# Linear attention and SwiGLU, two layers: half the one-column products, three weight loads spread out, an early silu table

## The chip, the cores and the metric

One core of a Trainium2 chip. The metric is the device time of one execution in microseconds. All arithmetic on TensorE is in pairs of 16-bit numbers (a high and a low part of each fp32 value), three matmuls for one product.

## The reference

x has 2048 rows (tokens) of 512. Two layers follow each other, with the same weights; each is

```python
x = x + A(layernorm(x))        # linear attention, 32 heads of 16
x = x + B(layernorm(x))        # out = (silu(x w1) * (x w3)) w2, F = 1792

# A:
phi = lambda t: where(t > 0, t + 1, exp(t)) + 1e-6
pq, pk = phi(q), phi(k)
kv = einsum("bhsd,bhse->bhde", pk, v);  z = sum of pk over the rows s
o  = (pq @ kv) / (pq . z + 1e-6)
return o @ wo
```

## The kernel before

The work goes through 16 token tiles of 128 rows. A layer has four stages.

*Keys* (the loop over t in `attention`). For each tile, `mm(pp, ...)` makes the keys (12 matmuls into the bank pk) from the transposed, normalised rows `xts[t]`; ACT and DVE make phi of it (`phi_act`, `phi_sum`), ACT rounds its high part (L942), DVE takes the low part (L957); and `gram(t)` adds rows-times-keys to four banks gt (12 matmuls). `keys_turn(t + 3)` splits the normalised rows of tile t + 3 (POOL or DVE, L1136) and has a DMA transpose write `xts[t + 3]` (L1137); `keep_transposed` stores one tile earlier to xt_d (L1155). POOL makes the layernorm's scale of tile t + 4.

*State*. The string `STATE[layer]` lists, in order, the steps between keys and queries: `totals` and `inverse` (the sum of the keys in the bank pz; its power-of-two inverse rz, L388), `gram_j` (gt times rz, L995, and its high part on ACT, L996), `low_j` and `lowp_j` (low parts on DVE or POOL, L999), `z` (zb, a scaled copy of pz, L1002), `col` (turns rows into columns by matmuls against a vector one_row that has a one in its first place, and makes from them the factor col), `kv`, `kvs` (kv masked and split, L1044 to L1054), `m_j` (kvs times wo, scaled by col, the weights that the queries' results meet; L1066, L1067), and the first queries `q_t`, `phi_t`, `in_t`, `out_t`.

*Queries*. The string `LOOP[layer]` lists the steps of each tile t from 0 to 13; `a` adds the attention's result to x and takes the row sums for the next layernorm (L1234, and on ACT L1238 and L1239). The last two tiles are added in the first group of the MLP.

*MLP*. Groups of Strassen-like products (banks ba, bb, bc), silu on ACT (L1288), the hidden values' parts, and products into the banks po. In layer 0 its idle slots also prepare the weights.

Between the layers (the seam), layer 1's first key tiles run among the last products of layer 0's MLP: `before_gram(t)` is `second(t)`, which for t = 0 and 1 closes the MLP, and at t = 1 loads layer 1's attention weights wv, wq and wo from att_d (1 MB each, L1705 to L1707).

The order on every engine is the order in which the code emits it (`in_order` pins PE, DVE, ACT, POOL and SP); every DMA goes through SP's one queue. ACT holds one set of functions at a time; exp and silu are in different sets, and the build puts an ACT_TABLE_LOAD ahead of the first activation that needs the other.

`f32()` hands out short-lived rows from a ring of four, in turn.

Of the kernel before, what the change touches and what calls it, by code (L numbers as in the profile page):

```python
# [11 lines left out]
AF = mybir.ActivationFunctionType  # L12
OP = mybir.AluOpType
# [4 lines left out]
P = 128  # L18
S, D, F, H = 2048, 512, 1792, 32
DH = D // H  # L20
NT, NC, NK, NF = S // P, S // 512, D // P, F // P
# [50 lines left out]
class Ring:  # L72
# [5 lines left out]
    def next(self, dtype, *dims):  # L78
        at = self.offsets[self.n % len(self.offsets)]
        self.n += 1  # L80
        return self.view(at, dtype, *dims)
# [7 lines left out]
def kernel(  # L89
# [10 lines left out]
    nc = tc.nc  # L100
# [10 lines left out]
    def view(at, dtype, *dims):  # L111
        size = 4 if dtype == F32 else 2
        n = size
        for d in dims:
            n *= d
        ap = arena[:, at // 4 : (at + n) // 4]
        if dtype != F32:
            ap = ap.bitcast(dtype)
        if len(dims) > 1:
            names = "abcdefg"[: len(dims)]  # L120
            ap = ap.rearrange(
                f"p ({' '.join(names)}) -> p {' '.join(names)}",
                **{n: d for n, d in zip(names[1:], dims[1:])},
            )
        return ap
# [36 lines left out]
    def f32(kind="short"):  # L162
        return ring[kind].next(F32, D)

    def later(n):
# [35 lines left out]
    LOADS = (  # L201
        (
            "q:2 b0:2 b1:3 b2:4 b3:5 v:6 o:7 b4:8 b5:9 b6:10 b7:11"
        ),
    )

    FIRST = (
# [14 lines left out]
    )  # L222
    LOOP = (
        (
            "f p i v f q w f o a"
        ),
        (
            "f p f q o i w v f a"
        ),
    )  # L230
    FILLS = (
# [76 lines left out]
    def scalar():  # L308
        i = next(column)
        return scalars[:, i : i + 1]  # L310

    one_row = scalar()
# [2 lines left out]
    small_eps = scalar()  # L315
    nc.vector.memset(small_eps, EPS * 2.0**-15)
    one_eps = scalar()
    nc.vector.memset(one_eps, 1.0 + EPS)

    mv_all = const.tile([P, NT, 2], F32, name="mv_all")  # L320
# [8 lines left out]
    wv_s = view(XB1, F16, 2, NK, D)  # L329
    wq_s = view(AT_H + 7 * KB, F16, 2, NK, D)  # L330
    wo_s = view(AT_H + 15 * KB, F16, 2, NK, D)
    g_s = view(XB0, F16, 2, NK, D)
    m_s = view(XB1, F16, 2, NK, D)
    zb = view(XB1 + 8 * KB, F32, D)
# [13 lines left out]
    att_d = {n: dram.tile([P, 2, NK, D], F16, name=f"{n}_d") for n in "kvqo"}  # L348
# [81 lines left out]
    def settle():  # L430
        while owed:
            owed.pop(0)()
# [12 lines left out]
    info = {}  # L445
# [434 lines left out]
    def attention(layer, ready, prep, before_gram):  # L880
# [5 lines left out]
        gt, pz, pks = [], [], {}  # L886
# [92 lines left out]
        held = {}  # L979
# [20 lines left out]

        def keep_z():
            nc.scalar.activation(zb, pz[0], AF.Copy, scale=info["itk"])  # L1002

        def columns():

            col = columns_
            for src, at in ((zb, 0), (held["rz"], 4)):
                for c in range(NK):
                    nc.tensor.matmul(
                        pz[0][:, at + c : at + c + 1],  # L1010
                        src[:, c * P : (c + 1) * P],
                        one_row,
                        start=True,
                        stop=True,
                    )
            held["col"] = col
            nc.vector.tensor_copy(col, pz[0][:, :4])
            nc.vector.scalar_tensor_tensor(
                col,
                col,  # L1020
                info["tk"],
                pz[0][:, 4:8],
                OP.mult,
                OP.mult,
            )
            nc.vector.reciprocal(col, col)
            nc.vector.tensor_scalar(col, col, 2.0**-17, None, op0=OP.mult)

        def kv_products():
# [26 lines left out]
        def out_weights(c):  # L1056
# [17 lines left out]
            "totals": totals,  # L1074
            "inverse": inverse,
            "z": keep_z,
            "col": columns,
            "kv": kv_products,
            "kvs": kv_parts,
# [16 lines left out]
        def out_of(t):  # L1096
            pos[t] = attn_out(t)

        ticks = {
            "q": lambda t: 4 < t + 4 < NT and query(t + 4),  # L1100
            "o": out_of,
# [3 lines left out]
            "a": lambda t: attn_add(t, pos.pop(t)),  # L1105
            "f": lambda t: fill(prep),
            "v": lambda t: settle(),
        }
        for t in range(NT - AFTER):
            next_tick(prep)  # L1110
# [60 lines left out]
    def query(t):  # L1171
        xt = xqs.pop(t)
        pp = acc_bank("pq") if t >= DEEP else bank("pq")
        mm(pp, lambda a, k: xt[:, a * NK + k, :], lambda b, k: wq_s[:, b, k, :], NK)
        pqs[t] = phi_act(pp, info["uq"], False, t >= DEEP)
        if t + 3 < NT:
            load_query(t + 3)
# [48 lines left out]
    def attn_out(t):  # L1226
        pt = pts.pop(t)
        po = bank("po")
        mm(po, lambda a, k: pt[:, a * NK + k, :], lambda b, k: m_s[:, b, k, :], NK)
        return po  # L1230
# [410 lines left out]
    for item in LOADS[0].split():  # L1641
        what, t = item.split(":")
# [58 lines left out]
    def second(t):  # L1701
        if t < 2:
            pending(t)
        if t == 1:
            nc.sync.dma_start(wv_s, att_d["v"])  # L1705
            nc.sync.dma_start(wq_s, att_d["q"])
            nc.sync.dma_start(wo_s, att_d["o"])  # L1707

    pair(1, nxt, None, second)


# [31 lines left out]
```

## Time and profile before

| | |
|---|---|
| time, median of 3 runs | 1192.5 us (1191.66 to 1192.67) |
| the profiled execution | 1187.6 us, span 1185.9 us |
| mean granted clock | 0.995 |
| matmuls (L1009) of the step `col`, recorded passes | 32 in both layers, median 250 ns each |
| ACT_TABLE_LOAD | 4, 1283 ns each; two of them at silu (L1288) |
| loads of wv, wq, wo, issue to landing | 7.4, 10.1 and 11.8 us |
| transposes of L1137, issue to landing | least 3.0, median 3.6, most 8.8 us |

Times are microseconds from the start of the span. PE is TensorE's matmuls, SPq the queue of DMA issues. A bracket at a timeline row gives how long the engine was idle before it and what it waited for. An fp32 matmul shows as two passes.

### The profile page before, as it was taken

What the parts mean: (1) busy time and instruction counts of PE and PEld (TensorE: products, weight loads), DVE (VectorE), ACT (ScalarE), POOL (GpSimd) and SP (SyncE); (2) the same over time, 40 slices, a digit from 0 to 9 for tenths busy, and PEclk for the clock granted to TensorE, in tenths of its full rate; (3) what the DMA queues carried; (4) which work ended last, traced back from release to release, by engine and by line L of the source; (5) the groups of instructions that cost most, each with busy time, mean ns of one, the idle gap of its engine ahead of it and who ended that gap; (6) DMA issues with size and microseconds to landing.
All of it is one profiled execution on the core that took longest, in us unless ns stands there. A gap on an engine that the chain in (4) does not pass through costs nothing.

```text
span 1185.9 us, 21854 instructions
## 1 busy us (share of the span) xinstructions
PE 1153.6 (97%) x8884; PEld 867.1 (73%) x8884; DVE 832.3 (70%) x1385; ACT 638.3 (54%) x1076; POOL 418.5 (35%) x488
## 2 busy tenths in 40 slices
PE   8999998899999999999998999999999999999998
PEld 3445444788888888888863454468888888888887
DVE  6788898977977896757774559747755775756543
ACT  5787687856554454334456644765544444444422
POOL 5342588302000134235267714684532200102010
PEclk9999999999999999999999999999999999999999
DMA  8986565979532221112226435664351350120010
GB/s 260 341 224 222 132 160 107 265 241 297 160 137 98 82 81 63 63 63 72 73 91 140 107 104 104 127 147 120 103 131 71 125 187 14 68 81 37 1 37 36
DMA packets 163396, 147.43 MB, mean 124 GB/s; under 512 B 129632, under 2 KB 138976, under 8 KB 158688
## 3 DMA queue, kind: packets, MB, share of 16 engines
q1 hardware_dynamic: 163296, 146.04, 42.7%
q8 instruction: 69, 1.13, 0.4%
q14 instruction: 31, 0.25, 0.1%
HBM read 72.48 MB, written 42.07 MB: 97 GB/s over the span
## 4 chain that ended last, share of the span: by engine, by line
PE 66%; DVE 12%; DMA 7%; POOL 6%; ACT 5%; issue 2%; SPq 1%; POOLq 0%; ACTq 0%; DVEq 0%
PE bb L514 17%; PE po L1380 13%; PE bc L514 9%; PE gt L514 6%; PE pk L514 5%; PE pq L514 4%; DMA arena<-arena 4%; PE ba L514 4%; PE po L514 3%; PE po L1400 3%; DMA arena<-in_B_w_dram 3%; DVE arena L1289 2%; DVE arena L1294 1%; DVE arena L1336 1%; DVE arena L1429 1%
## 5 line engine op out<-in xcount | busy, mean ns | idle before, releaser
L514 PEld LDWEIGHTS <-arena 128*128 128x128 f16 x6360 | 619.8, 98 | 261.6 <-issue 17.8
L514 PE MATMUL bb<-arena 128*128 128x256 f16 x2688 | 331.6, 274 | 7.9 <-ACT arena L1333 5.7
L1380 PE MATMUL po<-arena 128*128 128x256 f16 x1932 | 234.6, 273 | 6.8 <-ACT arena L1292 4.0
L1380 PEld LDWEIGHTS <-arena 128*128 128x128 f16 x1932 | 187.9, 98 | 33.0 <-ACT arena L1292 7.1
L1294 DVE TENSOR_TENSOR arena<-arena 128x512 f16<-128x512 f32 (+1 forms) x104 | 115.1, 1107 | 105.6 <-ACT arena L1292 105.3
L1333 ACT ACTIVATE arena<-bb 128x512 f32<-128x512 f32 x196 | 114.7, 589 | 124.7 <-PE bb L514 83.9
L514 PE MATMUL bc<-arena 128*128 128x256 f16 x1344 | 166.6, 273 | 2.5 <-ACT arena L1333 1.9
L1292 ACT ACTIVATE arena<-arena 128x512 f16<-128x512 f32 x112 | 99.8, 891 | 117.5 <-DVE arena L1307 44.9
L1288 ACT ACTIVATE arena<-arena,scalars 128x512 f32<-128x512 f32 x112 | 74.7, 667 | 116.0 <-DVE arena L1336 115.8
L1289 DVE SCALAR_TENSOR_TENSOR arena<-arena,scalars 128x512 f32<-128x512 f32 x112 | 87.7, 783 | 53.5 <-ACT arena L1288 53.4
L1336 DVE TENSOR_TENSOR arena<-arena,bc 128x512 f32<-128x512 f32 x112 | 76.3, 681 | 56.5 <-ACT arena L1333 46.4
L1449 POOL TENSOR_TENSOR arena<-arena 128x512 f32<-128x512 f32 x25 | 35.2, 1407 | 207.6 <-DVE arena L1429 207.6
L1429 DVE SCALAR_TENSOR_TENSOR arena<-po,scalars,arena 128x256 f32<-128x256 f32 (+1 forms) x170 | 92.0, 583 | 9.1 <-PE po L1380 7.6
L514 PE MATMUL pk<-arena 128*128 128x512 f16 x384 | 88.1, 379 | 3.5 <-DMA arena<-arena 3.3
L514 PE MATMUL po<-arena 128*128 128x512 f16 x384 | 87.8, 379 | 2.5 <-DMA arena<-arena 2.1
L514 PE MATMUL gt<-arena 128*128 128x512 f16 x384 | 89.5, 384 | 0.6 <-ACT arena L942 0.3
L514 PE MATMUL pq<-arena 128*128 128x512 f16 x384 | 87.6, 379 | 0.3 <-DVE arena L1067 0.2
L514 PE MATMUL ba<-arena 128*128 128x256 f16 x672 | 87.7, 274 | 0.0
L1304 POOL TENSOR_TENSOR arena<-arena 128x256 f32<-128x256 f32 x15 | 11.9, 791 | 148.3 <-DVE arena L1289 148.3
L491 ACT ACTIVATE arena<-arena,nb_all,rs_all 128x512 f32<-128x512 f32 x64 | 50.7, 807 | 24.5 <-POOL nb_all L488 22.8
L1400 PE MATMUL po<-arena 128*128 128x256 f16 x480 | 56.8, 273 | 0.6 <-DVE arena L1294 0.6
L1275 POOL TENSOR_TENSOR arena<-arena 128x512 f16<-128x512 f32 (+2 forms) x33 | 47.4, 1457 | 25.0 <-DMA arena<-arena 24.0
(163 smaller groups left out, 1291.2 us busy)
## 6 DMA issues: line engine op xcount, KB each, us to landing
arena<-xb_d SPq DMA_DIRECT2D x12, 1792.0 KB, 6.9
xb_d<-arena SPq DMA_DIRECT2D x8, 1792.0 KB, 5.9
xt_d<-arena SPq DMA_DIRECT2D x32, 256.0 KB, 3.2
arena<-xt_d SPq DMA_DIRECT2D x32, 256.0 KB, 3.2
arena<-in_B_w_dram SPq DMA_DIRECT2D x8, 896.0 KB, 6.9
arena<-in_B_w_dram SPq DMA_DIRECT2D x28, 256.0 KB, 3.4
w_d<-arena SPq DMA_DIRECT2D x4, 1792.0 KB, 10.3
arena<-w_d SPq DMA_DIRECT2D x4, 1792.0 KB, 6.7
```

What stands on the lines that cost most here:

```text
L491: nc.scalar.activation(dst, x_sb[:, t, :], AF.Identity, scale=rs_all[:, t : t + 1], bias=nb_all[:, t : t + 1],)
L514: nc.tensor.matmul(dst, lhs(a, k), rhs(b, k), start=first and k == 0 and i == 0, stop=last and k == n - 1 and i == len(PASSES) - 1, skip_g ...
L1275: engine_of("rowlow", 2 * c + j).tensor_tensor(nat[:, 1, lo:hi, :], s, nat[:, 0, lo:hi, :], OP.subtract)
L1288: nc.scalar.activation(t, gate, AF.Silu, scale=info["u1"])
L1289: nc.vector.scalar_tensor_tensor(t, up, info["hid"], t, OP.mult, OP.mult)
L1292: nc.scalar.activation(hs[:, 0, lo:hi], t[:, lo:hi], AF.Copy)
L1294: engine.tensor_tensor(hs[:, 1, lo:hi], t[:, lo:hi], hs[:, 0, lo:hi], OP.subtract)
L1333: nc.scalar.activation(dst, bank_, AF.Copy)
L1336: nc.vector.tensor_tensor(dst, dst, bank_, OP.add)
L1380: nc.tensor.matmul(po[:, i * HALF : (i + 1) * HALF], hs[:, a, qx, cs], w2[:, b, qw, :], start=g == ends[0] and i + a + b == 0, stop=g == e ...
L1400: nc.tensor.matmul(acc[n][:, half * HALF : (half + 1) * HALF], hs[:, a, qx, cs], w2_a21[g][:, b] if (i, half) == (0, 1) else w2[:, b, i + ...
L1429: nc.vector.scalar_tensor_tensor(dst, src, cb, to, OP.mult, OP.add)
```

## The change

Three edits.

1. The step `z` also multiplies pz by rz on DVE into a new row zr, and `col` takes the four columns of zr instead of four of zb and four of rz; the two small DVE operations that multiplied those go, and the reciprocal reads pz.
2. Layer 1's weights are no longer all loaded at t = 1, but wv at t = 1, wq at t = 3 and wo at t = 5.
3. The loop of the queries has a last step `x`, which at t = 12 runs silu on one column into a scalar that nothing reads.

```diff
     LOADS = (
         ...
+        (
+            "v:1 q:3 o:5"
+        ),
     LOOP = (
-            "f p i v f q w f o a"
+            "f p i v f q w f o a x"
         ...
-            "f p f q o i w v f a"
+            "f p f q o i w v f a x"
         ...
+    idle = scalar()
         ...
         def keep_z():
             nc.scalar.activation(zb, pz[0], AF.Copy, scale=info["itk"])
+            held["zr"] = f32()
+            nc.vector.tensor_tensor(held["zr"], pz[0], held["rz"], OP.mult)
 
         def columns():
             col = columns_
-            for src, at in ((zb, 0), (held["rz"], 4)):
-                for c in range(NK):
-                    nc.tensor.matmul(
-                        pz[0][:, at + c : at + c + 1],
-                        src[:, c * P : (c + 1) * P],
-                        one_row,
-                        start=True,
-                        stop=True,
-                    )
+            for c in range(NK):
+                nc.tensor.matmul(
+                    pz[0][:, c : c + 1],
+                    held["zr"][:, c * P : (c + 1) * P],
+                    one_row,
+                    start=True,
+                    stop=True,
+                )
             held["col"] = col
-            nc.vector.tensor_copy(col, pz[0][:, :4])
-            nc.vector.scalar_tensor_tensor(
-                col, col, info["tk"], pz[0][:, 4:8], OP.mult, OP.mult,
-            )
-            nc.vector.reciprocal(col, col)
+            nc.vector.reciprocal(col, pz[0][:, :NK])
             nc.vector.tensor_scalar(col, col, 2.0**-17, None, op0=OP.mult)
         ...
+        def silu_next():
+
+            nc.scalar.activation(idle, one_eps, AF.Silu)
+
         ticks = {
             ...
+            "x": lambda t: t == 12 and silu_next(),
         ...
     def second(t):
         if t < 2:
             pending(t)
-        if t == 1:
-            nc.sync.dma_start(wv_s, att_d["v"])
-            nc.sync.dma_start(wq_s, att_d["q"])
-            nc.sync.dma_start(wo_s, att_d["o"])
+        for item in LOADS[1].split():
+            what, at_ = item.split(":")
+            if int(at_) == t:
+                nc.sync.dma_start({"v": wv_s, "q": wq_s, "o": wo_s}[what], att_d[what])
```

SP's queue at the seam, before, from the store of tile 2's transposed rows on, with what each issue waits for (the names with HW are landings of earlier DMAs):

```order
L1155 DMA xt_d<-arena 128x1024 [waits DMAHW7_49,DMAHW4_49]
L1705 DMA arena<-v_d 128x4096
L1706 DMA arena<-q_d 128x4096 [waits DVE_49,PE_49]
L1707 DMA arena<-o_d 128x4096 [waits DMAHW2_49,DVE_49,PE_49]
L1137 DMA_TRANSPOSE arena<-arena 128x8x128 [waits DMAHW5_49,Pool_49]
L1155 DMA xt_d<-arena 128x1024 [waits DMAHW6_49]
```

The same place now, down to the transpose behind the third load:

```order
L1156 DMA xt_d<-arena 128x1024 [waits DMAHW7_49,DMAHW4_49]
L1708 DMA arena<-v_d 128x4096
L1138 DMA_TRANSPOSE arena<-arena 128x8x128 [waits DMAHW5_49,PE_49,Pool_49]
L1156 DMA xt_d<-arena 128x1024 [waits DMAHW6_49,DMAHW2_49]
L1138 DMA_TRANSPOSE arena<-arena 128x8x128 [waits DMAHW7_49,PE_49,Pool_49]
L1156 DMA xt_d<-arena 128x1024 [waits DMAHW1_49]
L1708 DMA arena<-q_d 128x4096 [waits DVE_49]
L1138 DMA_TRANSPOSE arena<-arena 128x8x128 [waits DMAHW2_49,PE_49,Pool_49]
L1156 DMA xt_d<-arena 128x1024 [waits DMAHW3_49]
L1138 DMA_TRANSPOSE arena<-arena 128x8x128 [waits DMAHW0_49,DMAHW4_49,PE_49,Pool_49]
L1156 DMA xt_d<-arena 128x1024 [waits DMAHW6_49]
L1708 DMA arena<-o_d 128x4096 [waits DVE_49]
```

The transposes of tiles 4 and 5 now stand ahead of the load of wq, those of tiles 6 and 7 between it and the load of wo.

DVE in layer 1's state, from the last product of the gram on (gt1 is one of the gram's banks, den the sums that the queries are divided by), before:

```order
L995 TENSOR_TENSOR arena_66<-gt1_6854,arena_66 128x512
L999 TENSOR_TENSOR arena_66<-arena_66 128x512
L877 SCALAR_TENSOR_TENSOR arena_66<-arena_66 128x512
L999 TENSOR_TENSOR arena_66<-arena_66 128x512 x2
L1190 SCALAR_TENSOR_TENSOR arena_66<-arena_66 128x512
L1192 TENSOR_REDUCE den_7580<-arena_66 128x32
L1207 TENSOR_SCALAR den_7580<-den_7580 128x32
L1208 RECIPROCAL den_7580<-den_7580 128x32
L1211 TENSOR_TENSOR arena_66<-arena_66,den_7580 128x512
L1017 COPY scalars_81<-pz_7465 128x4
L1018 SCALAR_TENSOR_TENSOR scalars_81<-scalars_81,pz_7465 128x4
L1026 RECIPROCAL scalars_81<-scalars_81 128x4
```

and now:

```order
L999 TENSOR_TENSOR arena_66<-gt1_6848,arena_66 128x512
L1003 TENSOR_TENSOR arena_66<-arena_66 128x512
L881 SCALAR_TENSOR_TENSOR arena_66<-arena_66 128x512
L1008 TENSOR_TENSOR arena_66<-pz_7461,arena_66 128x512
L1003 TENSOR_TENSOR arena_66<-arena_66 128x512 x2
L1191 SCALAR_TENSOR_TENSOR arena_66<-arena_66 128x512
L1193 TENSOR_REDUCE den_7577<-arena_66 128x32
L1208 TENSOR_SCALAR den_7577<-den_7577 128x32
L1209 RECIPROCAL den_7577<-den_7577 128x32
L1212 TENSOR_TENSOR arena_66<-arena_66,den_7577 128x512
L1022 RECIPROCAL scalars_81<-pz_7461 128x4
L1023 TENSOR_SCALAR scalars_81<-scalars_81 128x4
```

The product zr (L1008) has come in ahead of two low parts of the gram, and two small operations behind the columns are gone. In layer 0, where `z` is listed right behind `inverse`, L1008 stands ahead of the first product of the gram.

ACT in layer 1, around the first silu (L1288), before:

```order
L1238 ACTIVATE nm_all<-total 128x1
L1239 ACTIVATE arena,sq_all<-arena,nm_all 128x512
L1333 ACTIVATE arena<-bb 128x512
L1269 ACTIVATE arena<-arena 128x512
L1288 ACT_TABLE_LOAD
L1288 ACTIVATE arena<-arena,scalars 128x512
L1269 ACTIVATE arena<-arena 128x256
```

and ACT now, some ten activations earlier, around tile 12's statistics (L1239 and L1240 are the two lines of the statistics here, L495 the normalised rows of the MLP's next tokens):

```order
L1334 ACTIVATE arena<-bb 128x512
L1240 ACTIVATE arena,sq_all<-arena,nm_all 128x512
L1097 ACT_TABLE_LOAD
L1097 ACTIVATE scalars<-scalars 128x1
L1239 ACTIVATE nm_all<-total 128x1
L1240 ACTIVATE arena,sq_all<-arena,nm_all 128x512
L495 ACTIVATE arena<-arena,nb_all,rs_all 128x512
```

The load of the table has moved from just ahead of silu to behind tile 12's statistics, with the idle activation behind it, and nothing else on ACT has moved; the same holds in layer 0.

More of the change, by code (lines that the diff above doesn't have):

```diff
@@ L1002, in keep_z @@
             nc.scalar.activation(zb, pz[0], AF.Copy, scale=info["itk"])
+            held["zr"] = f32()
+            nc.vector.tensor_tensor(held["zr"], pz[0], held["rz"], OP.mult)
         def columns():
             col = columns_
-            for src, at in ((zb, 0), (held["rz"], 4)):
-                for c in range(NK):
-                    nc.tensor.matmul(
-                        pz[0][:, at + c : at + c + 1],
-                        src[:, c * P : (c + 1) * P],
-                        one_row,
-                        start=True,
-                        stop=True,
-                    )
-            held["col"] = col
[L1017 to L1024, printed above, removed]
-            )
-            nc.vector.reciprocal(col, col)
+            for c in range(NK):
[6 more added lines that the diff above has]
+                )
+            held["col"] = col
+            nc.vector.reciprocal(col, pz[0][:, :NK])
             nc.vector.tensor_scalar(col, col, 2.0**-17, None, op0=OP.mult)
```

## The prediction

> **What bounds the kernel now.** I read the page first, then the chain that ended last in order of time, then the timeline of the stretches that the change touches, and the busy table by small windows for the clock.
>
> ```profile
> PE 1153.6 (97%) x8884; PEld 867.1 (73%) x8884; DVE 832.3 (70%) x1385; ACT 638.3 (54%) x1076; POOL 418.5 (35%) x488
> ```
>
> TensorE is busy for 97% of the span, so a microsecond is gained only where PE stands still or where its own work shrinks. The change touches five such places, taken in order of size. Below, T4 is the transpose of token tile 4's normalised rows for layer 1's keys, pk4 the product that reads it, and so on.
>
> **1. The attention loads at the seam of the layers.** The timeline (start, length, engine), then two pieces of the chain (the second the pace of a product of 12 matmuls), then the landings: of the three loads (two shown), of all key transposes (L1137), and of the 1 MB load of wk (L1582).
>
> ```profile
> 615.33 0.44 SPq L1705 DMA_DIRECT2D arena<-v_d  x1
> 616.82 0.36 SPq L1707 DMA_DIRECT2D arena<-o_d  x1
> 620.78 1.86 SPq L1137 DMA_TRANSPOSE arena<-arena  x1
> 624.58 2.32 PE L514 MATMUL gt<-arena 128*128 128x512 f16 x10 [0.27 <-DVE arena L957]
> 625.57 2.97 SPq L1137 DMA_TRANSPOSE arena<-arena  x1
> 628.92 0.75 DVE L957 SCALAR_TENSOR_TENSOR arena<-arena,scalars 128x512 f16<-128x512 f32 x1 [1.96 <-ACT arena L942]
> 629.22 1.48 POOL L1136 TENSOR_TENSOR arena<-arena 128x512 f16<-128x512 f32 x1
> 629.65 2.76 PE L514 MATMUL pk<-arena 128*128 128x512 f16 x12 [2.76 <-DMA arena<-arena]
> ```
> ```profile
> 620.78 8.83 DMA arena<-arena
> ...
> 632.41 2.59 PE gt L514 x12
> ```
> ```profile
> arena<-v_d SPq DMA_DIRECT2D x1, 1024.0 KB, 7.4
> arena<-o_d SPq DMA_DIRECT2D x1, 1024.0 KB, 11.8
> ```
> ```profile
> DMA to landing us min/median/max: 3.0/3.6/8.8
> ```
> ```profile
> DMA to landing us min/median/max: 6.3/6.3/6.3
> ```
>
> Three loads of 1 MB go out within 1.5 us, the last landing at 616.82 + 11.8 = 628.6; T4, issued behind them at 620.78, lands at 629.61, and pk4 starts at 629.65 after an idle 2.76 us. With v alone ahead (landing at 615.33 + 7.4 = 622.7), T4 takes about its median 3.6 and lands at 624.4. PE is then still in gram 2, until 626.9, so pk4 starts at 626.9 and the whole 2.76 is free. Gram 3 (629.5) needs L957's low part by its third matmul; that ends at 629.67: no new wait worth counting. pk5 comes at 626.9 + 2 x 2.59 = 632.1, and T5 (issued 625.57, nothing heavy ahead any more) is there by 629.2.
>
> What is late next is T6. The q load now stands between T5's store and T6. I put its issue at about 627.4 (T5 and one store go out first), and it should land as wk's or v's did, 6.3 to 7.4 later: 633.7 to 634.8. T6 cannot be issued before POOL has its low part (629.22 + 1.48 = 630.7); T4 landed 1.0 after the load ahead of it, so T6 lands at 634.7 to 635.8. pk6 wants it at 632.1 + 2.59 = 634.7. New wait: 0 to 1.1, nearest the middle, 0.5. The o load goes out at t = 5, ahead of T8. At 4.5 us a tile from T6 I put T8's issue near 639.7; its product stands behind pk6, gram 4, pk7 and gram 5, at 634.7 + 4 x 2.59 = 645.1. That is 5.4 us of cover for a landing of 3.6 and a delay of about 1; without it, what exceeds 5.4 would be lost. Term: -2.76 + 0.5 = **-2.25** (ends -2.8 and -1.6).
>
> **2. The columns in layer 1.** Pieces of the chain, then timeline rows, then the price of an SBUF-PSUM product of the same shape as the added one.
>
> ```profile
> 705.88 1.75 PE pz L1009 x16
> 707.65 0.17 DVE scalars L1017
> 707.85 0.23 DVE scalars L1018
> 712.52 0.67 DVE arena L1067
> 713.23 2.75 PE pq L514 x12
> ```
> ```profile
> 701.14 2.25 DVE L999 TENSOR_TENSOR arena<-arena 128x512 f16<-128x512 f32 x2
> 703.04 2.84 PE L514 MATMUL kv<-arena 128*128 128x128 f16 x48
> ```
> ```profile
> L995 DVE TENSOR_TENSOR arena<-gt,arena x8: 677/680/693, 110.1 to 698.0; 128x512 f32<-128x512 f32 x8
> ```
>
> Eight one-column products take 16 passes and 1.75 us; four take 0.87. Of the four small DVE operations behind them, L1017 and L1018 go: 0.17 + 0.23 and their two gaps, 0.45. All of it is on the chain down to L1067, which frees the bank of the next pq. So L1067 ends 1.32 earlier, at 711.87, and PE, itself 0.87 ahead, gets through pq and pm at 705.88 + 0.88 + 2 x 2.59 = 711.94. The next pq starts there instead of at 713.23: **-1.28**.
>
> Added: one DVE product, 0.68, between phi_0 and the two low parts of L999. They end at 703.39 now; POOL's fourth low part shares their time, and behind a 0.68 delay the second would run mostly without it, ending near 703.7. kv's twelfth matmul, the first that reads it, comes at 703.04 + 11 x 0.059 = 703.7 (48 take 2.84). So kv's leading matmuls hide it; without that cover it costs at most 0.68 - 0.3 = 0.4. Ends -1.4 and -0.9.
>
> **3. The columns in layer 0.** The chain's piece, then the timeline.
>
> ```profile
> 113.22 1.68 PE pz L1009 x16
> ```
> ```profile
> 114.56 1.24 POOL L999 TENSOR_TENSOR arena<-arena 128x512 f16<-128x512 f32 x1 [0.33 <-ACT arena L996]
> 119.05 0.35 DVE L1208 RECIPROCAL den<-den 128x32 f32<-128x32 f32 x1 [1.32 <-ACT den L1194]
> 189.43 2.76 PE L514 MATMUL po<-arena 128*128 128x512 f16 x12 [1.40 <-DMA arena<-arena]
> ```
>
> Half of 1.68 is 0.84 of PE, and PE runs without a gap from there to 188. The added 0.68 stands ahead of gram_0 here, so the last low part of the gram ends at up to 115.8 + 0.7 = 116.5, just ahead of kv's new start (113.22 + 0.84 + 2.59 = 116.65); DVE's later path has 1.32 of idle before L1208. Hence 0.84 goes down the chain; at 189.43 PE waits on a DMA that hangs on POOL, whose chain starts from the same place. Nothing there has a fixed time, but many engines are close: **-0.8**, ends -0.9 and 0.
>
> **4. Silu's table in layer 1.** The timeline, then the one-column activations of L1238 (ns: least, median, most), the nearest thing to the idle one.
>
> ```profile
> 788.05 0.60 ACT L1333 ACTIVATE arena<-bb 128x512 f32<-128x512 f32 x1 [0.79 <-PE bb L514]
> 795.84 1.28 ACT L1288 ACT_TABLE_LOAD   x1
> 799.02 0.57 ACT L1333 ACTIVATE arena<-bb 128x512 f32<-128x512 f32 x1
> 799.64 1.47 PE L514 MATMUL bc<-arena 128*128 128x256 f16 x12 [1.94 <-ACT arena L1333]
> 804.97 0.94 ACT L1269 ACTIVATE arena<-arena 128x512 f16<-128x512 f32 x2 [2.35 <-DMA arena<-arena]
> ```
> ```profile
> L1238 ACT ACTIVATE nm_all<-total x32: 186/198/203, 134.9 to 792.0; 128x1 f32<-128x1 f32 x32
> ```
>
> The load delays L1333 at 799.02, for which PE stands idle 1.94. Without it the copy ends 1.28 earlier and PE waits 0.66: **-1.28**. The end on the weak side is -0.5, if ACT's next wait (804.97, on a transpose) does not move along; that transpose is issued by ACT's own earlier work, so it should. On the strong side -1.5. The load reappears behind tile 12's statistics, 4 to 5 us before 788.05, with a one-column activation of about 0.20: 1.48 in all. ACT's idle of 0.79 takes up half of it, and what is left, up to 0.7, falls on a copy that PE does not wait for (its next bb product stands behind a po).
>
> The Trainium skill (ScalarE: Activation LUTs, What ACT_TABLE_LOAD costs) counts about 1.38 us of drain with each 1.28 us load. By it this term would be -1.94, all of PE's wait, and the sum -6.3; the trace shows no drain: the load runs from 795.84 and silu's first activation starts at 797.14.
>
> **5. Silu's table in layer 0.**
>
> ```profile
> 205.23 0.60 ACT L1333 ACTIVATE arena<-bb 128x512 f32<-128x512 f32 x1 [0.57 <-POOL arena L1219]
> 206.63 1.33 ACT L436 ACTIVATE arena<-arena,scalars 128x512 f16<-128x512 f32 x2 [0.81 <-POOL arena L570]
> 209.06 2.75 PE L514 MATMUL po<-arena 128*128 128x512 f16 x12 [0.41 <-DVE arena L1234]
> 212.27 1.28 ACT L1288 ACT_TABLE_LOAD   x1
> ```
>
> The load leaves 212.27, where PE does not wait, and enters near 202.6. ACT's idle of 0.57 and 0.81 takes up 1.38 of the 1.48; but VectorE waits for the normalised rows in between, and PE at 209.06 waits for VectorE. Ends: +1.5 if all of that reaches PE, -1.3 if what follows 212.27 hung on ACT. I take **0**, since the waits behind (226 to 232) are for DMA.
>
> **Sum.** -2.25 - 1.28 - 0.8 - 1.28 + 0 = -5.6. The profiled execution took 1187.6 us (span 1185.9) and would take 1182.0. It lies 4.9 below the median of the three runs, 1192.5, so against the median I predict 1186.9. About 0.2% (2.4 us) is what a measurement of this kernel can tell from no change.
>
> **Rivals.**
>
> (a) *The clock falls elsewhere.* Rows of the timeline and of the busy table (after the counts: granted clock, DMA share, GB/s):
>
> ```profile
> 198.14 2.29 PE L514 MATMUL bb<-arena 128*128 128x256 f16 x10 [2.07 <-DMA arena<-arena]
> ```
> ```profile
> 199.00:200.00 1.00, 1.00 (x6) 0.71 (x5) 0.20 (x2) 0.77 (x2) 1.00 (x2) 0.50 0.75 139
> 629.60:630.60 1.00, 0.95 (x5) 0.48 (x6) 0.08 (x1) 0.00 (x0) 1.00 (x1) 1.00 2.40 106
> ```
>
> After 2.07 us of idle the clock is halved (10 matmuls take 2.09 instead of 1.09), until about 201.7: some 1.7 us lost. After 2.76 us of idle at the seam it stays at 1.00. So a shift of layer 0 by less than a microsecond may win or lose such a stretch: 1185.2 or 1188.6. The Trainium skill (TensorE: Matmul & The Clock Gate, What's actually happening) has the gate close after a free-running idle window of about 3.4 us; by that rule neither pause would do it, and the first did, so here a pause can cost more than the page allows. Chance 0.2, both ways together.
>
> (b) *The gains do not add.* T6 waits its full 1.1, layer 1's table gain ends at the transpose at 804.97 (-0.5), and layer 0 gives nothing back because VectorE is late at 209 (+1.0): -1.6 - 1.0 - 0.5 + 1.0 - 0.4 = -2.5, that is 1190.0; a little worse and it is within 0.2%. For it: PE hardly waits in layer 0's attention, so its pace there may be POOL's. Chance 0.14.
>
> (c) *Slower.* Each load alone holds its transpose as three held T4, 8.83. T6 would land at 630.7 + 8.8 = 639.5, 4.8 late, and T8, two tiles on, some 3.4 late again; with two halved clock stretches at 1.7 that is +11.6 against -2.76 saved and -3.4 elsewhere: 1198. It decides from a landing of T6 after about 640. Against it: 1 MB alone landed in 6.3. Chance 0.05.
>
> My forecast as it stands: 0.61. The range takes in (a) and most of (b), on the near side the strong ends (-2.8 - 1.4 - 0.9 - 1.5 - 1.3 = -7.9) and a saved clock stretch: 1181.5 to 1191.5. Faster by over 0.2%: 0.61 + 0.2 and a little of (b), 0.82; same 0.13; slower 0.05.
>
> **What would show it.** T4 landing near 624.4 on the old time scale, and pk4 without a wait on DMA; pk6 with a wait of 0 to 1.1. Eight passes of L1009's kind per layer, the reciprocal straight behind them, and the pq after pm 1.3 earlier relative to kv. No table load between the first silu and its predecessor, PE's wait at 799.64 down to about 0.7. Wrong would be: pk6 or pk8 waiting over 2 us; kv waiting for a low part; PE's wait at 209 grown past 1.5; a third stretch of half clock.

## The result and the profile after

The changed kernel took 1181.63 us (median of 4 executions, 1180.77 to 1184.08) against 1192.08 of the kernel before (4 executions, 1191.4 to 1192.67): ratio 0.9916, 95% interval 0.9899 to 0.9933. Measured again in a later series it took 1183.21 us (5 executions) against 1190.16 (20 executions): 0.9944, 0.9930 to 0.9959. In the three later series, each on a chip of its own and 78 executions together, the kernel before had medians of 1189.54, 1190.16 and 1188.88, and single executions from 1184.47 to 1195.57. Its first four (on three of which the forecast of 1186.9 was built) thus lay in the upper part of its own spread, so of the first difference of 10.5 us some 7 are the change's. The profiled executions are 1187.6 and 1182.41 us: 5.2 less, where 5.6 were forecast. One slow execution of the unchanged kernel, 6111.9 us in `same` below, is in no figure here.

Of the changed kernel: the busy line of the page, the loads of layer 1's attention weights in the DMA view (KB and us to landing), and the landings of the key transposes (now L1138) in the view of that line:

```profile
PE 1148.0 (97%) x8868; PEld 863.3 (73%) x8868; DVE 831.0 (70%) x1383; ACT 638.8 (54%) x1078; POOL 420.6 (36%) x488
```
```profile
arena<-v_d SPq DMA_DIRECT2D x1, 1024.0 KB, 6.9
arena<-q_d SPq DMA_DIRECT2D x1, 1024.0 KB, 5.5
arena<-o_d SPq DMA_DIRECT2D x1, 1024.0 KB, 5.9
```
```profile
DMA to landing us min/median/max: 3.0/3.1/9.2
```

TensorE is as full as before and has 16 passes fewer; the loads of 1 MB land after 5.5 to 6.9 us, where the three together took 7.4 to 11.8. The longest of the transposes, 9.2, was issued at 570.67, ahead of these loads.

To see where the 5.2 us are, I divided both profiled executions at starts of TensorE's rows:

| piece of the span | before | changed | difference | forecast |
|---|---|---|---|---|
| start to layer 0's first queries (pq) | 107.88 | 109.69 | +1.81 | none |
| layer 0: first pq to kv (columns) | 9.47 | 8.57 | -0.90 | -0.84 |
| kv to the pq behind the first m | 8.15 | 8.65 | +0.50 | 0 |
| from there to the po near 556 (queries, first MLP groups) | 431.03 | 429.29 | -1.74 | 0 |
| to layer 1's first keys (pk) | 30.68 | 30.67 | 0 | 0 |
| layer 1's keys, the seam in them, to the sum of the keys (pz, the step `totals`) | 107.20 | 104.37 | -2.83 | -2.25 |
| layer 1's state and queries, to the first bb of its MLP | 86.16 | 85.34 | -0.82 | -1.28 |
| to the end (silu's table) | 405.33 | 404.12 | -1.21 | -1.28 |

**The seam.** SP's queue and then TensorE, by the timeline of the changed kernel:

```profile
615.04 0.44 SPq L1708 DMA_DIRECT2D arena<-v_d  x1
620.49 1.24 SPq L1138 DMA_TRANSPOSE arena<-arena  x1
627.69 0.42 SPq L1708 DMA_DIRECT2D arena<-q_d  x1
630.46 1.23 SPq L1138 DMA_TRANSPOSE arena<-arena  x1
```
```profile
624.29 2.32 PE L518 MATMUL gt<-arena 128*128 128x512 f16 x10 [0.27 <-DVE arena L961]
626.45 2.75 PE L518 MATMUL pk<-arena 128*128 128x512 f16 x12
629.04 2.75 PE L518 MATMUL gt<-arena 128*128 128x512 f16 x12
631.63 5.38 PE L518 MATMUL pk<-arena 128*128 128x512 f16 x24
```

pk4 (626.45) follows gram 2 without a wait: the 2.76 us are gone. The q load goes out at 627.69, near the forecast 627.4, and lands after 5.5 us, at 633.2, where the forecast took 6.3 to 7.4. T6, issued at 630.46, lands 1.0 behind it (after 3.7 us, at 634.2), just when pk6 wants it (631.63 + 2.59); pk5 and pk6 stand in one row of 24 matmuls without a bracket, so the new wait of 0 to 1.1 on T6 is 0 here. The margin is thin: in a second profile of this kernel (`after2`) pk6 starts 0.33 late.

**The columns, layer 1.** The chain:

```profile
698.28 0.59 ACT arena L1006
698.87 0.02 issue
698.90 0.69 DVE arena L1008
699.59 1.21 DVE arena L1003 x2
700.80 0.04 issue
700.84 2.23 PE kv L518 x37
703.07 0.85 PE pz L1014 x8
...
703.95 0.19 DVE scalars L1022
```

Eight passes in 0.85 us and the reciprocal straight behind them, as forecast. New on the chain is ACT's copy zb (L1006) with zr (L1008) behind it and the two low parts (L1003) behind that: kv now waits for these, and it takes 0.35 us longer from its start to the columns (3.03 instead of 2.68). Layer 0, where kv's row breaks in two, by the timeline, and the group of zr:

```profile
112.64 0.69 DVE L1008 TENSOR_TENSOR arena<-pz,arena 128x512 f32<-128x512 f32 x1 [0.84 <-ACT arena L1006]
118.26 0.44 PE L518 MATMUL kv<-arena 128*128 128x128 f16 x5
119.00 2.56 PE L518 MATMUL kv<-arena 128*128 128x128 f16 x43 [0.29 <-POOL arena L1003]
```
```profile
its engine sat idle before it (us, times) until:
  ACT arena L1006: 1.7, 2
```

zr only reads pz, and so does zb; still VectorE stands idle until ACT's copy has ended, 0.84 us in each layer.

**Silu's table, layer 1.** ACT and then TensorE, by the timeline:

```profile
779.61 1.28 ACT L1097 ACT_TABLE_LOAD   x1
780.90 0.20 ACT L1097 ACTIVATE scalars<-scalars 128x1 f32<-128x1 f32 x1
...
794.22 1.47 PE L518 MATMUL bc<-arena 128*128 128x256 f16 x12 [0.51 <-ACT arena L1334]
802.98 1.59 PE L1381 MATMUL po<-arena 128*128 128x256 f16 x13 [1.83 <-ACT arena L1293]
```

The wait at bc is 0.51 instead of 1.94. At the po it is 1.83, where before waits of 1.17 and 0.31 stood just before and at that po, so 0.35 is given back.

**Silu's table, layer 0.** The same two engines:

```profile
204.09 1.28 ACT L1097 ACT_TABLE_LOAD   x1
208.14 1.47 PE L518 MATMUL bb<-arena 128*128 128x256 f16 x12 [1.01 <-ACT arena L1334]
210.78 2.75 PE L518 MATMUL po<-arena 128*128 128x512 f16 x12 [1.16 <-DVE arena L1235]
```

Here a bb that had no wait before waits 1.01, and the po behind it 1.16 instead of 0.41. That is not the price of the edit. In the kernel before, the clock had been halved just ahead, from 198 on, and so TensorE came late to this po and waited little. Where the clock held there, a kernel without layer 0's idle silu waits 1.7 us at the same po; this is `all_silu1` of experiment 3:

```profile
210.75 2.75 PE L515 MATMUL po<-arena 128*128 128x512 f16 x12 [1.71 <-DVE arena L1232]
```

At the next bb (211.65 in the kernel before), counted from layer 0's pq behind the first m, the six profiles with this idle silu are 0.26 to 0.31 us behind the kernel before and the seven others without it 0.02 to 0.12. So the price here is some 0.3 us, and the half clock at 198 had cost nothing by then. Yet the whole piece is 1.74 shorter; experiments 3 and 4 show why.

### The profile page after: what moved, and what is told of

It reads as the page before. It is cut to its first block, busy times and chain, and to the rows that moved or that the text cites. A ratio compares the mean times of both kernels' runs of the same rounds, so it can differ in the third digit from the quotient of the medians.

```text
span 1180.7 us, 21818 instructions
## 1 busy us (share of the span) xinstructions
PE 1148.0 (97%) x8868; PEld 863.3 (73%) x8868; DVE 831.0 (70%) x1383; ACT 638.8 (54%) x1078; POOL 420.6 (36%) x488
## 4 chain that ended last, share of the span: by engine, by line
PE 60%; DVE 15%; ACT 7%; POOL 6%; DMA 6%; issue 3%; SPq 1%; POOLq 0%; ACTq 0%; DVEq 0%
PE bb L518 16%; PE po L1381 13%; PE bc L518 8%; PE gt L518 5%; PE pk L518 5%; PE ba L518 4%; PE po L518 3%; PE pq L518 3%; DMA arena<-arena 3%; DMA arena<-in_B_w_dram 3%; PE po L1401 2%; DVE arena L1290 2%; DVE arena L1337 2%; DVE arena L442 2%; DVE arena L1430 2%
## 5 line engine op out<-in xcount | busy, mean ns | idle before, releaser
L1289 ACT ACTIVATE arena<-arena,scalars 128x512 f32<-128x512 f32 x112 | 74.7, 667 | 116.0 <-DVE arena L1337 115.5
L495 ACT ACTIVATE arena<-arena,nb_all,rs_all 128x512 f32<-128x512 f32 x64 | 50.5, 807 | 26.5 <-POOL nb_all L492 26.3
```

What stands on the lines that cost most here:

```text
L495: nc.scalar.activation(dst, x_sb[:, t, :], AF.Identity, scale=rs_all[:, t : t + 1], bias=nb_all[:, t : t + 1],)
L1289: nc.scalar.activation(t, gate, AF.Silu, scale=info["u1"])
```

## The experiments

Each kernel was timed against the kernel before in the same series. A ratio can differ a little from the quotient of the two medians, by 0.1% at most (`all_swap`); where they disagree, the ratio with its interval is the measurement.

**1. The same kernel and its three edits, each alone** (one chip, before 1189.54). `same` is the kernel before, unchanged:

> The kernel before, unchanged, profiled and timed again. Theory A (the sum): its traces differ from the first one only by chance, and its time is the 1192 of the runs. Theory B (the clock): the first profiled execution, 1187.6, is low because it lost fewer half-clock stretches than most; this profile shows three or more of them between 100 and 830 us where the first had two (at 198 and 232), and its time is nearer 1192 for it. If the profile again takes 1187 to 1188 while the timed runs take 1192, the gap is one between profiled and timed executions and not the clock.

`loads` is edit 2 alone:

```diff
         if t == 1:
             nc.sync.dma_start(wv_s, att_d["v"])
+        if t == 3:
             nc.sync.dma_start(wq_s, att_d["q"])
+        if t == 5:
             nc.sync.dma_start(wo_s, att_d["o"])
```

> The loads of wv, wq and wo at t = 1, 3 and 5, nothing else. Theory A: pk4 starts after gram 2 without a wait on a DMA, pk6 waits 0 to 1.1, and the time falls by 2.3 to 2.9. Theory B: where the pause of 2.76 us at the seam also costs a half-clock stretch in most executions of the kernel before, the time falls by 4 to 4.6 instead.

`cols` is edit 1 alone (zr, four columns, the reciprocal of pz):

```diff
+            held["zr"] = f32()
+            nc.vector.tensor_tensor(held["zr"], pz[0], held["rz"], OP.mult)
         ...
-            for src, at in ((zb, 0), (held["rz"], 4)):
         ...
+            for c in range(NK):
         ...
```

> Half the one-column products, with the product zr on VectorE, in both layers, nothing else. Theory A: 1.28 in layer 1 and 0.8 in layer 0, in all -2.1. Rival: in layer 0 the added product delays the gram's low parts and kv, so layer 0 gives nothing or loses up to 1, and the time falls by 0.3 to 1.3. Theory B: 1.7 more or less with each stretch of half clock that the shift moves.

`silu` is edit 3 alone, in both layers:

```diff
         ...
+            "x": lambda t: t == 12 and silu_next(),
         ...
```

> Silu's table brought in at t = 12 by the idle activation in both layers, nothing else. Theory A: layer 1 gains 1.28, layer 0 nothing: -1.3. Rival: in layer 0 PE's wait near 209 for VectorE grows from 0.41 to 1 to 2, and the time falls by 0 to 0.5. Theory B: the longer waits near 208 move or add a half-clock stretch, 1.7 either way.

| kernel | median us | ratio, 95% interval | mean granted clock of all its executions |
|---|---|---|---|
| before, in this series (29) | 1189.54 | | 0.9964 |
| `same` (11) | 1189.66 | 1.0002, 0.9989 to 1.0015 | 0.9975 |
| `loads` (5) | 1184.66 | 0.9963, 0.9951 to 0.9975 | 0.9980 |
| `cols` (11) | 1190.52 | 1.0007, 0.9995 to 1.0020 | 0.9956 |
| `silu` (11) | 1187.08 | 0.9977, 0.9968 to 0.9986 | 0.9975 |

By the medians the loads give the most, 4.9 us (4.4 by the ratio); silu's table 2.5 (2.7), twice the 1.3 expected; the columns nothing, where 2.1 were expected, though they shorten both layers' states. The three together give 6.4 (4.9 + 2.5 - 1.0), about the 7 of the whole change. The unchanged kernel came out at 1189.66, not near the 1192 that was expected of it, and its profile (1190.99 us) has one half-clock stretch between 100 and 830 us (at 630), where the first profile (1187.6) has two: such stretches are not why the first profile was the lower one.

The loads give more than their pause. The keys of layer 1 with the seam took 107.20, 106.98, 107.25 and 105.72 us in four profiles with the old loads (before, `silu1`, `cols`, `silu0`), 108.88, 109.13 and 108.76 in three more (`same`, `silu`, `cols_swap`), and 104.27 to 104.66 in the six with the loads apart. Two things part the first two groups. The pause ahead of pk4 differs from execution to execution: it is 2.76, 2.52, 2.79 and 1.27 us in the four, and 3.15, 3.32 and 2.94 in the three. And behind the three the clock is halved, by the timeline of `same` and its busy table (after the counts: granted clock, DMA share, GB/s):

```profile
631.08 4.05 PE L514 MATMUL pk<-arena 128*128 128x512 f16 x12 [3.15 <-DMA arena<-arena]
```
```profile
630.00:631.00 1.00, 0.00 (x0) 0.00 (x0) 0.72 (x1) 0.00 (x0) 0.92 (x2) 0.66 1.19 366
631.00:632.00 1.00, 0.92 (x3) 0.37 (x4) 0.00 (x0) 0.00 (x0) 0.92 (x2) 0.50 2.52 126
...
633.00:634.00 1.00, 1.00 (x4) 0.40 (x3) 0.00 (x0) 0.00 (x0) 1.00 (x2) 0.63 1.04 340
```

pk4's 12 matmuls take 4.05 instead of 2.75 (4.13 in the other two) because the clock is halved from 630.3 to 633.7. So by these profiles the edit is worth 106.8 - 104.4 = 2.4 where the clock held, near the 2.25 forecast, and 108.9 - 104.4 = 4.5 where it fell; of the 2.1 between, 0.8 is the longer pause (means of 3.1 and 2.3 us) and 1.3 the half clock. Over all seven the mean is 3.3, and the ratio's interval, 3.0 to 5.8 us, takes that in.

**2. The pause kept, TensorE kept busy in it.** `fill` is the kernel before with ten idle matmuls into a bank of its own ahead of pk4:

```diff
+            if layer == 1 and t == 4:
+                spare = bank("spare").rearrange("p (a n) -> p a n", a=4)
+                for _ in range(10):
+                    wide = ones16[:, None, :].to_broadcast([P, 4, P])
+                    nc.tensor.matmul(spare, ones16, wide, start=True, stop=True)
```

> The kernel before with ten idle matmuls (2.2 us, into a spare bank) on TensorE ahead of pk4, inside its pause at the seam; no other work moves. Theory B (a pause costs a half-clock stretch, 1.7, in those executions in which more than about 2 us of it fall into one window of a free-running clock of 3.4 us): pk4 starts when T4 lands, as before, no half clock near 630, and the time is 0.8 to 1.3 lower. Rival (the pause costs only itself): the same time within 0.4.

Measured: 1189.08 us (12 executions) against 1190.16, ratio 0.9997, 0.9986 to 1.0008. The timeline:

```profile
626.03 2.32 PE L927 MATMUL spare<-ones 128*128 128x512 f16 x10
629.38 2.76 PE L514 MATMUL pk<-arena 128*128 128x512 f16 x12 [1.03 <-DMA arena<-arena]
```

pk4 runs at full clock here, though without the idle matmuls the pause would have been 1.0 + 2.2 = 3.2 us, as long as those behind which it fell. The time does not show it. By experiment 1's profiles, three half clocks of 1.3 us in seven would be worth 0.6; the interval, -1.7 to +1.0 us, takes that in and zero as well. What the clock at the seam is worth on average is not shown.

**3. The changed kernel again, with layer 0's idle silu taken out, and with zr ahead of zb** (the chip of `fill`). `after2` is the changed kernel:

> The changed kernel again, timed beside the others. Theory A (the parts add as the runs of the parts alone showed: loads -4.4, columns about 0, silu -2.7): the time is 6 to 7.5 below the kernel before on this chip. Rival (the first comparison is the rule): 9 to 11 below.

`all_silu1` leaves out the step x in layer 0:

```diff
-            "f p i v f q w f o a x"
+            "f p i v f q w f o a"
```

> The changed kernel with the idle activation in layer 1 alone; layer 0 loads silu's table where it did before. Theory A (layer 0's part is worth nothing): the same time as the changed kernel within 0.5. Rival 1 (layer 0's part is a loss, PE waits about 2.2 near 208 in the changed kernel against 0.4 to 1.7): 0.5 to 1.5 faster. Rival 2 (it is a gain, since PE's wait near 232 shrank from 2.3 to 1.6 and half-clock stretches there are rarer): 0.5 to 1.5 slower.

`all_swap` has the product zr ahead of the copy zb:

```diff
-            nc.scalar.activation(zb, pz[0], AF.Copy, scale=info["itk"])
             held["zr"] = f32()
             nc.vector.tensor_tensor(held["zr"], pz[0], held["rz"], OP.mult)
+            nc.scalar.activation(zb, pz[0], AF.Copy, scale=info["itk"])
```

> The changed kernel with zr computed on VectorE ahead of ACT's copy zb, so that VectorE no longer waits 0.84 for ACT before zr. Theory A (that wait is what cost the columns most of their gain): in layer 0 kv no longer waits for POOL's low part and the stretch from kv to the pq behind pm is 8.2 as before the change, in layer 1 the next pq starts 1.1 to 1.3 earlier than before the change instead of 0.8; 0.6 to 1 faster than the changed kernel. Rival (it is the 0.68 of work on VectorE, not the wait): those stretches stay at 8.65 and -0.8.

Measured: `after2` 1183.21 us (5 executions), 0.9944 (0.9930 to 0.9959); `all_silu1` 1186.31 (8), 0.9972 (0.9961 to 0.9983); `all_swap` 1180.17 (5), 0.9926 (0.9911 to 0.9940). Layer 0's idle silu, which the forecast put at nothing, is thus worth 0.28% between `all_silu1` and `after2`, 3.1 us by the medians, and the intervals do not meet. `all_swap` lies 0.18% below `after2`, more than the 0.6 to 1 us expected, but there the intervals overlap.

**4. The parts of which that is made** (a third chip, before 1188.88). `silu0` and `silu1` have the step x in layer 0 or in layer 1 alone, and nothing else (the string is that of `silu0`):

```diff
     LOOP = (
-            "f p i v f q w f o a"
+            "f p i v f q w f o a x"
```

> The kernel before with the idle silu in layer 0 alone. Theory A (what the traces of the other versions show: with the idle silu in layer 0 the idle time of TensorE ahead of the bb product near 232 is 1.3 to 1.8 us, without it 2.2 to 3.7 us, and only the longer one is followed by half clock): 1.0 to 3.0 us less than before, ratio 0.9975 to 0.9992, with that wait under 1.9 us and no half clock at 232 in the profile. Theory B (the prediction's term 5): 0, ratio 0.9995 to 1.0005, since the waits from 226 to 232 hang on DMA. Theory C: the load falls on VectorE's path at 209 and costs up to 1.5 us, ratio up to 1.0013.

> The kernel before with the idle silu in layer 1 alone. Prediction's term 4: 1.3 us less, ratio 0.9989, the wait at the bc product behind the first silu from 1.94 to about 0.6 us. Rival: the gain is lost again at the next po (wait 1.83 there in the changed kernel, where 1.17 and 0.31 stood before), 0.9 us less, ratio 0.9992. If layer 0's and layer 1's parts add up, this and the one in layer 0 alone together give the 0.23% that both together gave.

`cols_swap` is `cols` with zr ahead of zb:

> The kernel before with the columns' edit alone, and DVE's product zr ahead of ACT's copy zb of the same bank instead of behind it. Theory A (zr's 0.84 us wait for ACT delays the low parts that kv reads): against the columns' edit alone kv has no wait for a low part, 0.46 us less from the first kv matmul to the first m matmul in layer 0 and 0.1 us less in layer 1, so 1.8 us less than before in all, ratio 0.9985. Rival (the bank, not the order, holds kv up): the waits stay, ratio that of the edit alone, 0.9995 to 1.002, and 5.73 us from kv to m in layer 0.

`all_swap2` is `all_swap` once more:

> The changed kernel with zr ahead of zb, a second time, on another chip or at another time. If the first measurement (0.9926, 0.9911 to 0.9940) tells a real gain over the changed kernel (0.9944, 0.9930 to 0.9959, on the same chip), the ratio is again 0.991 to 0.994, 0.6 us below what the changed kernel's parts give; if it was the spread of half clock stretches between executions, it may come out anywhere from 0.991 to 0.996.

| kernel | median us | ratio, 95% interval | mean granted clock |
|---|---|---|---|
| before, in this series (29) | 1188.88 | | 0.9973 |
| `silu0` (11) | 1187.66 | 0.9997, 0.9985 to 1.0009 | 0.9966 |
| `silu1` (12) | 1188.26 | 0.9995, 0.9980 to 1.0009 | 0.9972 |
| `cols_swap` (12) | 1190.83 | 1.0018, 1.0002 to 1.0034 | 0.9950 |
| `all_swap2` (6) | 1181.08 | 0.9939, 0.9924 to 0.9953 | 0.9985 |

Neither half of edit 3 shows by itself; the 1.0 to 3.0 us expected of `silu0` did not come, and its profile has 2.29 us of wait and a half clock at 233. The two halves' sum, 0.08%, and the 0.23% of both together differ by no more than the intervals. The columns' edit with zr first made the kernel slower, if barely clear of the noise, where 1.8 us less was expected. So the worth of layer 0's idle silu depends on the columns. One stretch of the trace shows how: from layer 0's pq behind the first m to the po near 556, one profile for each kernel:

| | columns as before | columns by half |
|---|---|---|
| silu as before | before 431.0, `same` 429.3, `loads` 430.1, `fill` 430.5, `silu1` 429.7: mean 430.1 | `cols` 434.0, `cols_swap` 434.1, `all_silu1` 433.5: mean 433.9 |
| idle silu in layer 0 | `silu0` 430.2, `silu` 428.4: mean 429.3 | changed 429.3, `after2` 429.8, `all_swap` 430.1, `all_swap2` 428.9: mean 429.5 |

With the columns alone 3.8 us are lost in this stretch, more than they gain anywhere, and the idle silu takes that back; by itself it brings 0.8, less than single profiles differ. Most of it happens near 232. At the po that starts at 222.13 in the kernel before, all profiles still stand within some 0.3 us of it, counted from the start of the stretch. At the po near 236 the means against the kernel before are -0.7 with neither edit, +1.7 with the columns alone, -1.4 with the idle silu alone and -2.5 with both. The rest falls mainly behind 300, where the kernels with the columns lose some 1 us whether they have the idle silu or not; it was not traced. SP's queue, ACT and TensorE near 232, by the timelines, first of `cols`:

```profile
224.13 1.52 SPq L1270 DMA_TRANSPOSE arena<-arena  x1
225.80 2.03 SPq L538 DMA_DIRECT2D arena<-in_B_w_dram  x3
231.13 0.51 ACT L436 ACTIVATE arena<-arena,scalars 128x256 f16<-128x256 f32 x1 [4.43 <-DMA arena<-in_B_w_dram]
233.82 2.72 PE L514 MATMUL bb<-arena 128*128 128x256 f16 x12 [4.37 <-ACT arena L1325]
```

then of the kernel before, with TensorE's po for the place in the program:

```profile
222.13 2.56 PE L1400 MATMUL po<-arena 128*128 128x256 f16 x22
224.31 1.52 SPq L1278 DMA_TRANSPOSE arena<-arena  x1
225.97 2.05 SPq L538 DMA_DIRECT2D arena<-in_B_w_dram  x3
229.25 0.51 ACT L436 ACTIVATE arena<-arena,scalars 128x256 f16<-128x256 f32 x1 [2.38 <-DMA arena<-in_B_w_dram]
231.95 2.44 PE L514 MATMUL bb<-arena 128*128 128x256 f16 x12 [2.33 <-ACT arena L1333]
```

and of the changed kernel:

```profile
223.62 1.52 SPq L1279 DMA_TRANSPOSE arena<-arena  x1
223.84 2.56 PE L1401 MATMUL po<-arena 128*128 128x256 f16 x22
225.29 2.01 SPq L542 DMA_DIRECT2D arena<-in_B_w_dram  x3
229.14 0.51 ACT L440 ACTIVATE arena<-arena,scalars 128x256 f16<-128x256 f32 x1
232.15 1.47 PE L518 MATMUL bb<-arena 128*128 128x256 f16 x12 [1.59 <-ACT arena L1334]
```

ACT's copy, for which bb waits, stands behind its split of a weight piece (L436), and that waits for the piece's landing. The pieces go out on SP behind a transpose of the low parts of the MLP's next rows (L1278 in the kernel before, L1270 in `cols`, L1279 in the changed kernel). VectorE makes these low parts, and in its order they stand behind its product with silu (L1289). Without layer 0's idle silu VectorE waits there for ACT, which loads the table at 212. VectorE in `all_silu1` and in `after2`, which differ in nothing else:

```profile
216.02 0.76 DVE L1287 SCALAR_TENSOR_TENSOR arena<-arena,scalars 128x512 f32<-128x512 f32 x1 [0.60 <-ACT arena L1286]
```
```profile
215.63 0.75 DVE L1290 SCALAR_TENSOR_TENSOR arena<-arena,scalars 128x512 f32<-128x512 f32 x1
```

This wait of 0.5 to 0.6 us, and a second one of 0.3 to 0.4 behind it, is in all eight profiles without layer 0's idle silu and in none of the six with it. So without it the pieces go out 3.7 to 3.9 us behind the start of that po (225.97 - 222.13; 5.0 in `fill`), with it 1.4 (225.29 - 223.84, and in `silu`) or 2.1 (in the four others). Then ACT's split has no wait in the changed kernel, and bb waits 1.3 to 1.6 in the four profiles with both edits, against 3.7 to 4.4 in the three with the columns alone and 2.2 to 3.1 in the five with neither. After the shortest of these waits the clock held each time, after the longest it was halved each time, and between them now and then: bb's 12 matmuls take 2.72 in `cols`, 2.44 in the kernel before and 1.47 in the changed one.

With the columns alone a piece needs 4.6 to 5.3 us from issue to ACT's row in three profiles, with neither edit 2.9 to 3.8 in five. What the pieces meet there was not looked at further and stays open.

Swapping zr and zb does in layer 0 what it was to do, by the timeline of `all_swap2`:

```profile
118.66 2.84 PE L518 MATMUL kv<-arena 128*128 128x128 f16 x48
```

kv is in one row again; from kv to the first m layer 0 takes 5.27 instead of 5.73 us, as before the change, in all three kernels with the swap. In layer 1 it takes 6.37 instead of 6.49 us, and the pq behind pm starts 0.94 earlier than before the change instead of 0.82, where 1.1 to 1.3 were expected. There zr does start earlier, but the two low parts behind it take 2.09 us in `all_swap` instead of 1.28: they run beside POOL's low part (699.42 to 700.58), which in the changed kernel has ended when they begin. So in layer 1 the rival named for `all_swap` was nearly right. That POOL's work is what slows them is not tested; the overlap is what the timelines show. The medians with the whole change, 1180.17 and 1181.08 us, are the lowest of all kernels here. That this version also beats the changed kernel rests on these 0.46 + 0.12 = 0.58 us; the ratios' intervals overlap.

## Why the prediction was right and where it was not

The direction and the range held; the forecast of -5.6 for the profiled execution met -5.2. Both numbers owe something to luck. The -5.2 contains +1.81 that no edit touches and -1.74 in a stretch that was forecast at 0, so the sum came out through errors that cancelled. The first median, 1181.63, lies 0.13 inside the near end of the range, 1181.5, and the terms named for that end give only 1192.5 - 7.9 - 1.7 = 1182.9. The order of the parts did not hold: the columns of both layers were to give 2.1, more than silu's table, and gave nothing in the time.

- **Seam, -2.25.** The mechanism was right to the row: pk4 without a wait, T6 as forecast in place. The mis-sized term is T6's wait: taken as 0.5, measured 0 (0.33 in `after2`), since the q load landed in 5.5 us. The edit was worth 2.4 in the profiles where the clock held (2.83 between the two profiled executions). Not in the term: the pause varied from 1.27 to 3.32 us, and the three longest of seven were followed by half clock, another 1.3 us each. The prediction read "at the seam it stays at 1.00" from one execution as if it were fixed.
- **Columns in layer 1, -1.28.** Measured -0.82. The passes and the small operations went as priced. The step that failed is "kv's leading matmuls hide it": the low parts that kv reads end 0.56 later (from the sum of the keys on) instead of 0.3, and of the missing 0.46 kv loses 0.35. zr was taken as 0.68 of VectorE, yet it also waits 0.84 for ACT's copy of the same bank; the order of the instructions showed the two reads of pz next to each other. But the wait is not the whole cause here: with zr first, kv to m is only 0.12 shorter, for the low parts then take 0.8 longer (beside POOL's, experiment 4). A kv that waits for a low part was named as a sign of being wrong, and it came, by 0.29 and 0.20.
- **Columns in layer 0, -0.8.** Measured -0.90 + 0.50 = -0.4 for the state: with the 0.84 of waiting, POOL's last low part ends 1.34 later instead of up to 0.7, and kv waits for it. Here the swap gives back all of the 0.50. Further down, "0.84 goes down the chain" failed: it held to the po near 222, and then, without the idle silu, 2.4 us were lost near 232 and 3.8 by 556. So 0 was no bound on the weak side; a loss of some 3 was possible. In the time, `cols` (both layers) came out at 1.0007, no change, and `cols_swap` at 1.0018.
- **Silu's table in layer 1, -1.28.** Measured -1.21 here and -1.44 between the means of seven profiles each with and without it (404.19 and 405.63 from the first bb to the end). Right; no drain showed, as the prediction had it: the idle activation starts 0.01 us behind the load. By itself in the time it could not be seen (0.9995, 0.9980 to 1.0009).
- **Silu's table in layer 0, 0.** The failed step: "the waits behind (226 to 232) are for DMA", read as independent of ACT. They are for DMA, but those DMAs stand on SP's queue behind a transpose that waits for VectorE, and VectorE waits for silu. The edit is worth 3.1 us where the columns are halved, and about 0.8 by the means of the stretch where they are not. Of the price feared at 209, up to 1.5, some 0.3 came and is contained in these. PE's waits there sum to more than 1.5 (1.01 + 1.16), which was to be a sign of being wrong; but the 0.41 it was measured against stood behind a half clock, and without one the wait is 1.7 before the change too.
- **Rival (a), the clock falls elsewhere.** It had 0.2 for both signs, and it is a real part of the result. The mean granted clock of the kernel before was 0.9969 over its 78 executions, that of the changed kernel 0.9990 over 9. The difference of 0.0021 is at most 0.0021 x 1185 = 2.5 us of the 7, if TensorE had work all that time. It had not always: the half clock at 198, priced at 1.7, was made up at the next wait. In `cols` (0.9956) and `cols_swap` (0.9950) the clock went the other way.
- **Rival (b), the gains do not add.** It spoke of late waits that eat gains. They do not add, but the other way: the idle silu in layer 0, which shows nothing by itself (0.9997), takes 3.1 us off once the columns are halved.
- **Rival (c), T6 and T8 held.** Not seen; no pk behind the loads waits for more than the 0.33 us of `after2`.

The profiled execution of the changed kernel also lost 1.81 ahead of all this, in a wait for a DMA near 45 that differs from execution to execution (0.55 to 3.1 us in these profiles) and was followed by half clock. No edit touches that place.

## What to carry to other kernels

When a wait is put down to a DMA, look up where that DMA was issued and what stood ahead of it on its queue: a change on another engine may set it. A faster step ahead of an engine that is paced by something else only makes the next wait longer, and in these profiles a pause of some 2 us was now and then followed by half clock, up to 1.7 us of work more; so price edits in pairs, and judge a clock from several executions. Ahead of a new read of a bank, see which engine reads it just then: here the second reader waited, and the order of the two reads was free to choose. A wait taken from one profile may be short only because a half clock stood ahead of it.

## What the runs showed of the hardware

Two reads of one bank by two engines came one after the other: zr (VectorE) waited 0.84 us for ACT's copy, in both layers. With zr first VectorE has no wait, and ACT's copy waits for zr (0.41 us in layer 1 of `all_swap`).

Most pauses after which the clock was halved were 1.9 to 4.4 us long (the shortest, at 19 in `cols`, was 1.6 us with another 0.4 just behind it), and pauses of the same length were spared in other executions: 2.07 at 198 in the kernel before was followed by half clock, 2.07 at the same place in the changed kernel was not, nor 3.05 at 232 in `fill`. At the seam the three pauses that were followed by it were the longest of seven, yet length alone does not decide. The half clock lasted about 3.4 us (630.3 to 633.7 above), some 1.7 us of work, and twice as long behind the 4.37 in `cols`. Where a wait was due behind it, less was lost, or nothing: the one at 198 in the kernel before was made up by 212, and in `silu0` the clock was halved at 800 and two later waits, of 1.17 and 0.31 in the kernel before, were gone, so the piece to the end took 405.3 us in both.
